# Score products of an attention kernel in four 64x64 array tiles instead of two 64x128 tiles

## The chip, the cores and the metric

The kernel runs on one core of one Trainium2 chip. The metric is the device time of one execution in microseconds (us), lower is better. The core has a matrix engine (TensorE, PE in the profile, with its weight loads listed apart as PEld), three engines for elementwise work (VectorE or DVE, ScalarE or ACT, GpSimd or POOL) and SyncE (SP), which issues DMAs. A matmul on TensorE uses two instructions: a weight load, which puts the stationary operand into the array, and the matmul itself, which streams the moving operand past it. Results go to PSUM.

## The reference

Attention with a sliding window of 128 positions and a linear distance bias, for 8 batches, 8 heads, 576 positions and head size 64; then layer norm, a two-layer MLP and a residual sum:

```python
scores = (1 / sqrt(64)) * q @ k.T                 # per batch and head, 576 x 576
scores = where(0 <= rel < 128, scores - slope[h] * abs(rel), -1e9)
attn = softmax(scores)
x = (attn @ v) with heads joined                  # 8 x 576 x 512
xn = (x - mean) / sqrt(var + 1e-6) * g_ln
out = x + maximum(xn @ w_ch1, 0) @ w_ch2          # 512 -> 2048 -> 512
```

All inputs and the output are fp32; the kernel computes in fp16 with fp32 sums.

## The kernel before

The 8 x 576 positions are cut into 36 blocks of 128 rows. `attention(i)` does one block: it loads q, k and v as fp16 (casting DMAs from the GpSimd queue), turns q and k so that the head's 64 elements lie on partitions (`qkt`, tiles of 128 partitions x 2 x 4 x 128: two heads lie above one another, one on partitions 0 to 63, the other on 64 to 127, and four such pairs side by side), makes the scores (`e_s`, L732), takes their exponent on ScalarE out of PSUM (`e_x`, L780), masks them on VectorE (`e_m`, L787), multiplies with v (`e_pv`, L808, 65 columns: 64 of v and one of ones for the sum) and normalises on VectorE (L825, L829). Because of the window, a block's queries see only the keys of their own block and of the one before, so the scores of a block are 8 heads x 2 key blocks = 16 products of 128 keys x 128 queries with a contraction of 64. Blocks that start a batch have no block before and make 8.

The scores are written turned, keys on the partitions: the weights are 128 keys of one head (64 rows x 128 columns), the moving operand is the 128 queries of that head, and the result fills 128 partitions of the score tile. The two score tiles (`sc0`, `sc1`, two PSUM banks each) take four heads each. The innermost loop goes over the two heads `g` of a pair: their operands lie on different halves of the partitions, and their results in different PSUM banks. For the first five blocks the distance bias is laid into PSUM by a matmul first (`e_z`, L748) and the score product adds to it (`start=not bias`); later blocks multiply with a mask table instead.

`mlp(c)` does the MLP for chunks of two or four blocks: the first layer at L1210 (at L1121 for the last two chunks), the second at L1247 for the first four chunks and at L992 for the others; L1121 and L992 follow a scheme with fewer products and more sums. Both use the four general PSUM tiles `fb`.

The order of all work is written out by hand: `ORDER` (L119 to L210) is a list of task names with the engine and the PSUM tile of each, `plan.run()` turns it into a list of closures, and each engine executes its share in that order. `S7:T0` in it is the score task of block 7 on TensorE. A score task holds all 16 products of a block (`Sa` and `Sb` hold half each for the first two blocks); score tasks stand between MLP tasks and value tasks (`pva`, `pvb`), so that the score matmuls come in short blocks among others. Waits are placed by the framework: a score task waits for the turned q and k (for most blocks a transposing DMA on SyncE's queue, L710) and for ScalarE to have read the score tile of the block before. `keep_warm` (L1287) puts in idle matmuls at the start.

Of the kernel before, what the change touches and what calls it, by code (L numbers as in the profile page):

```python
# [213 lines left out]
def kernel(  # L214
# [10 lines left out]
    nc = tc.nc  # L225
    B, H, S, D = q.shape
# [3 lines left out]
    P = 128  # L230
# [57 lines left out]
    def ring(name, n, shape, dt, pinned=()):  # L288
        return plan.ring([sb(f"{name}{i}", shape, dt) for i in range(n)], {k: sb(f"{name}p{k}", shape, dt) for k in pinned})
# [20 lines left out]
    qkt = ring("qkt", 6, [P, 2, HP, P], FP16, FAR)  # L310
# [33 lines left out]
    scs = [spsum.tile([P, 2, 512], FP32, tag=f"sc{n}", name=f"sc{n}") for n in range(2)]  # L344
# [216 lines left out]
    def attention(i):  # L561
# [4 lines left out]
        bias = i < BY_BIAS  # L566
# [155 lines left out]
        def e_s(halves):  # L722
            def emit(e, b):
                for half in halves:
                    for slot in range(2):
                        hp = 2 * half + slot
                        for side in (() if r == 0 else (0,)) + (1,):
                            for g in range(2):
                                rows = slice(D * g, D * g + D)
                                kt = qkt[i if side else before]  # L730
                                c0 = slot * 2 * P + side * P
                                nc.tensor.matmul(  # L732
                                    scs[half][:, g, c0 : c0 + P],
                                    kt[rows, 1, hp, :],
                                    qkt[i][rows, 0, hp, :],
                                    start=not bias,
                                    stop=True,
                                    skip_group_check=True,
                                )
            return emit  # L740

        def e_z(halves):
# [587 lines left out]
```

## Time and profile before

| What | us |
|---|---|
| Median of 3 runs (lowest, highest) | 300.7 (299.6, 300.96) |
| The profiled execution, whole | 300.98 |
| Its span from first to last instruction | 299.1 |
| VectorE busy | 242.8 |
| ScalarE busy | 165.3 |
| GpSimd busy | 105.4 |
| L732 weight loads, busy | 14.9 + 2.3 |

The page of a profile gives the busy time of each engine, the chain of work that ended last (followed back from the last instruction to what released each step), and groups of instructions by source line: how many, how long they kept the engine busy together, and the mean duration of one. Matmuls are pipelined: one of 128 columns is listed with 216 ns, but the next can start 56 ns behind it. So durations of single matmuls do not add up, and the steps between their starts are what tells the cost. A timeline row gives the start, the length and the number of instructions that were merged into it. The granted TensorE clock is full from 14.5 us of the span on; between 11.1 and 14.5 us it is half.

The 16 DMA engines are busy for nine tenths of the time or more in nearly every slice until about 190 us of the span, for the most part with the casting loads.

### The profile page before, as it was taken

The numbers are of one execution on the slowest core, as the hardware profiler recorded it, in microseconds if no ns is written. First come the engines' busy times: TensorE is split into PE (matmuls) and PEld (weight loads), VectorE is DVE, ScalarE is ACT, GpSimd is POOL, SyncE is SP. The second block draws the span as 40 slices with busy tenths as digits, with TensorE's granted clock in tenths as the row PEclk, the third lists the DMA queues.
The fourth block names the chain that finished last, engine by engine and source line by source line (L and its number), as shares of the span: only waits on it lengthen the run. The fifth ranks groups of instructions, "written<-read, shape, count | busy, mean of one in ns | idle before, by whom it ended". The sixth has DMA issues, their size and how long they took to land.

```text
span 299.1 us, 7458 instructions
## 1 busy us (share of the span) xinstructions
PE 293.3 (98%) x3014; PEld 225.1 (75%) x3014; DVE 242.8 (81%) x583; ACT 165.3 (55%) x273; POOL 105.4 (35%) x138
## 2 busy tenths in 40 slices
PE   8999999999999999899999999999999999999995
PEld 8789756875955578566886588657787799999984
DVE  3397289998879879849978888788899988988983
ACT  3664536794798573368528444676544655245500
POOL 5965369738137428433633567300000000000000
PEclk9799999999999999999999999999999999999999
DMA  6999999999999999999999999968101033012015
GB/s 179 159 196 194 206 144 141 146 138 133 122 219 145 151 224 133 145 140 167 179 166 197 182 159 143 158 171 150 36 19 55 0 125 89 2 37 106 35 55 193
DMA packets 163779, 39.93 MB, mean 133 GB/s; under 512 B 154017, under 2 KB 159137, under 8 KB 163746
## 3 DMA queue, kind: packets, MB, share of 16 engines
q0 software_dynamic: 110000, 17.70, 95.6%
q1 hardware_dynamic: 53744, 21.77, 40.5%
q8 instruction: 23, 0.38, 0.6%
q14 instruction: 10, 0.08, 0.1%
q10 hardware_dynamic: 2, 0.00, 0.0%
HBM read 36.70 MB, written 9.44 MB: 154 GB/s over the span
## 4 chain that ended last, share of the span: by engine, by line
PE 94%; DMA 4%; DVE 1%; ACT 0%; issue 0%
PE fb L1210 32%; PE fb L992 27%; PE fb L1247 9%; PE u L1121 8%; PE sc L732 6%; PE fb L808 6%; DMA qkt<-qk 4%; PE fb L1287 2%; PE sc L748 1%; PE fb L695 1%; PE fb L440 0%; PE fb L906 0%; PE fb L426 0%; DVE ot L1004 0%; DVE xb L829 0%; ACT probs L780 0%
## 5 line engine op out<-in xcount | busy, mean ns | idle before, releaser
L1210 PE MATMUL fb<-xt,w1sb 128*128 128x512 f16 (+1 forms) x576 | 106.4, 332 | 0.6 <-DMA xt<-xs 0.6
L780 ACT ACTIVATE probs<-sc 128x1024 f16<-128x1024 f32 (+1 forms) x72 | 67.4, 975 | 36.0 <-PE sc L732 27.3
L1210 PEld LDWEIGHTS <-w1sb 128*128 128x128 f16 x576 | 61.5, 114 | 27.8 <-DMA xt<-xs 0.9
L1227 ACT ACTIVATE ht<-fb 128x512 f16<-128x512 f32 x88 | 51.1, 598 | 44.4 <-PE fb L1210 44.2
L992 PEld LDWEIGHTS <-ht 128*128 128x128 f16 x560 | 53.2, 98 | 9.2
L496 POOL DMA_DIRECT2D qk<-in_k_dram x38 | 32.8, 866 | 44.3 <-DMA qkt<-qk 36.8
L992 PE MATMUL fb<-w2sb,ht 128*128 128x256 f16 x336 | 44.7, 273 | 0.0
L496 POOL DMA_DIRECT2D qk<-in_q_dram x38 | 32.5, 861 | 16.6 <-DMA qkt<-qk 9.6
L496 POOL DMA_DIRECT2D vx<-in_v_dram x36 | 31.0, 868 | 15.6 <-PE fb L808 12.4
L787 DVE TENSOR_TENSOR probs<-probs,mreg 128x1024 f16<-128x1024 f16 (+1 forms) x46 | 30.4, 667 | 1.1 <-ACT probs L780 1.0
L992 PE MATMUL fb<-ks,ht 128*128 128x256 f16 x224 | 30.8, 273 | 0.0
L1247 PE MATMUL fb<-w2sb,ht 128*128 128x512 f16 x128 | 30.7, 379 | 0.0
L829 DVE SCALAR_TENSOR_TENSOR xb<-fb,rec 128x256 f16<-128x256 f32 x72 | 29.5, 416 | 0.9
L808 PEld LDWEIGHTS <-probs 128*128 128x128 f16 x544 | 23.9, 98 | 6.8
L808 PE MATMUL fb<-vx,probs 128*128 128x65 f16 x496 | 26.1, 194 | 0.0
L1004 DVE TENSOR_TENSOR ot<-fb,xb 128x512 f32<-128x512 f32 (+1 forms) x31 | 19.6, 634 | 6.0 <-PE fb L992 5.6
L848 DVE BATCH_NORM_STATS2 st<-xb 128x6 f32<-128x512 f16 x36 | 24.2, 682 | 0.2
L825 DVE RECIPROCAL rec<-fb 128x4 f32<-128x4 f32 x72 | 12.2, 174 | 14.7 <-PE fb L808 12.4
L1225 DVE TENSOR_SCALAR ht<-fb 128x512 f16<-128x512 f32 x24 | 16.0, 681 | 8.4 <-PE fb L1210 8.3
L1247 PEld LDWEIGHTS <-ht 128*128 128x128 f16 x128 | 11.6, 98 | 11.1
L732 PEld LDWEIGHTS <-qkt 64*128 64x128 f16 x496 | 14.9, 94 | 6.4 <-issue 5.3
L1144 DVE TENSOR_TENSOR ht<-u,probs 128x512 f16<-128x512 f32 x24 | 16.2, 685 | 2.7 <-PE u L1121 1.8
(113 smaller groups left out, 387.7 us busy)
## 6 DMA issues: line engine op xcount, KB each, us to landing
out_dram<-ot SPq DMA_DIRECT2D x32, 256.0 KB, 2.9
qk<-in_q_dram POOLq DMA_DIRECT2D x30, 128.0 KB, 7.6
qk<-in_k_dram POOLq DMA_DIRECT2D x30, 128.0 KB, 7.2
vx<-in_v_dram POOLq DMA_DIRECT2D x28, 128.0 KB, 7.7
w1sb<-in_moe_w_ch_dram POOLq DMA_DIRECT2D x4, 512.0 KB, 9.1
w2sb<-in_moe_w_ch_dram POOLq DMA_DIRECT2D x4, 512.0 KB, 14.1
out_dram<-ot SPq DMA_DIRECT2D x8, 128.0 KB, 1.8
qs<-in_q_dram SPq DMA_DIRECT2D x2, 256.0 KB, 3.6
```

What stands on the lines that cost most here:

```text
L496: nc.gpsimd.dma_start(out=dst(p0, n), in_=src[b, :, s0 : s0 + n, :].rearrange("h p d -> p h d"))
L732: nc.tensor.matmul(scs[half][:, g, c0 : c0 + P], kt[rows, 1, hp, :], qkt[i][rows, 0, hp, :], start=not bias, stop=True, skip_group_check=True,
L780: nc.scalar.activation(out=o, in_=n_, func=AF.Exp, scale=inv_sqrt_d)
L787: en.tensor_tensor(out=pv, in0=pv, in1=mask[:, 2 * half : 2 * half + 2, :, lo:], op=ALU.mult)
L808: nc.tensor.matmul(pp[:, hh * (D + 1) : hh * (D + 1) + D + 1], probs[i][:, bank, slot, side * P : side * P + P], vx[i if side else before] ...
L829: nc.vector.scalar_tensor_tensor(out=xb[c][:, j, 256 * half : 256 * half + 256].rearrange("p (h d) -> p h d", d=D), in0=pp[:, :, 0:D], sca ...
L848: nc.vector.bn_stats(out=st[i][:, :], in_=xb[c][:, j, :])
L992: nc.tensor.matmul(o, lhs(f, p), rhs(f), start=first and f == 0 and (p == 0 or key[0] != key[1]), stop=f == F2 - 1, skip_group_check=True)
L1121: nc.tensor.matmul(late[bank][:, FOURTH * f : FOURTH * f + FOURTH], w, rhs[kb], start=first and f == kb == 0, stop=kb == 1, skip_group_che ...
L1210: nc.tensor.matmul(fb[b][:, n_ * x : n_ * x + n_], w1f[f // CB][:, kb, (f + x) % CB, :], xt[c][:, kb, 0:n_], start=(kb == x == 0), stop=(k ...
L1227: nc.scalar.activation(out=o, in_=src, func=AF.Relu)
L1247: nc.tensor.matmul(pm[:, 0 : c1 - c0], ht[c][:, f, j * P : j * P + P], w2sb[f // CB][:, f % CB, c0:c1], start=(f == 0), stop=(f == NFB - 1),)
```

## The change

The weights of one score product, 64 rows x 128 key columns, are loaded and used in two halves of 64 key columns. Each half is a matmul of its own with the same moving operand (the head's 128 queries), and writes 64 of the 128 result partitions. With the two heads of a pair that makes four products on four 64x64 quarters of the array: rows 0 to 63 or 64 to 127 by the head, columns 0 to 63 or 64 to 127 by the half of the keys. Their order is head 0 low keys, head 0 high keys, head 1 low keys, head 1 high keys. 544 score matmuls and as many weight loads become 1088 of each; results, tiles, waits and the order of the tasks stay.

```diff
                                 c0 = slot * 2 * P + side * P
-                                nc.tensor.matmul(
-                                    scs[half][:, g, c0 : c0 + P],
-                                    kt[rows, 1, hp, :],
-                                    qkt[i][rows, 0, hp, :],
-                                    start=not bias,
-                                    stop=True,
-                                    skip_group_check=True,
-                                )
+                                for z in range(2):
+                                    nc.tensor.matmul(
+                                        scs[half][D * z : D * z + D, g, c0 : c0 + P],
+                                        kt[rows, 1, hp, D * z : D * z + D],
+                                        qkt[i][rows, 0, hp, :],
+                                        start=not bias,
+                                        stop=True,
+                                        skip_group_check=True,
+                                    )
```

`D` is 64 and `P` is 128.

## Prediction

> **What bounds the kernel now.** I read the busy shares first, then the chain that ended last, then TensorE's own waits, then the score products' line.
>
> ```profile
> PE 293.3 (98%) x3014; PEld 225.1 (75%) x3014; DVE 242.8 (81%) x583; ACT 165.3 (55%) x273; POOL 105.4 (35%) x138
> ...
> PE 94%; DMA 4%; DVE 1%; ACT 0%; issue 0%
> PE fb L1210 32%; PE fb L992 27%; PE fb L1247 9%; PE u L1121 8%; PE sc L732 6%; PE fb L808 6%; DMA qkt<-qk 4%; PE fb L1287 2%; PE sc L748 1%; PE fb L695 1%; PE fb L440 0%; PE fb L906 0%; PE fb L426 0%; DVE ot L1004 0%; DVE xb L829 0%; ACT probs L780 0%
> ```
>
> The page says that TensorE sets the end: 94% of the chain is matmuls, and L732, the score products, is 6% of it. TensorE executes in order, so what is added to one matmul group moves everything behind it, unless a wait swallows it. There is little to swallow it:
>
> ```profile
> PE fb L1287 <- DVE warm_t L387: 1.1, 1, 1.1
> PE fb L1210 <- DMA xt<-xs: 0.6, 1, 0.6
> PE sc L732 <- DMA qkt<-qk: 0.5, 1, 0.5
> PE fb L1287 <- DVE xb L829: 0.3, 1, 0.3
> ```
>
> These are TensorE's waits (total us, times, longest). The first lies ahead of any score product. Only the 0.5 us, at 125.1 us of the span, and the 0.6 us could absorb something. So a longer score block costs nearly its full length.
>
> One score block in the timeline (start us, us, what):
>
> ```profile
> 131.53 0.65 PE L808 MATMUL fb<-vx,probs 128*128 128x65 f16 x16
> 132.11 0.23 PE L732 MATMUL sc<-qkt,qkt 64*128 64x128 f16 x2
> 132.17 0.22 PE L732 MATMUL sc<-qkt 64*128 64x128 f16 x2
> 132.23 0.22 PE L732 MATMUL sc<-qkt,qkt 64*128 64x128 f16 x2
> ...
> 132.51 0.22 PE L732 MATMUL sc<-qkt 64*128 64x128 f16 x2
> 132.66 0.62 PE L1210 MATMUL fb<-xt,w1sb 128*128 128x512 f16 x2
> ```
>
> The two matmuls of a row (the two heads, rows 0-63 and 64-127) start together, 3 to 4 ns apart by the trace's start times, and the rows are 56 ns apart. So two 64x128 tiles already run side by side, and a pair costs one stream of 128 columns: 56 ns, which is 2.4 columns per ns plus a little over 2 ns. There are 544 such matmuls, that is 272 pairs, 15.2 us, in 37 blocks (31 of 16 matmuls, the rest of 4, 8 or 12). Around each block the trace has two gaps: 123 ns from the last L808 matmul to the first L732 one, where the L808 matmuls are 29 ns apart, so 94 ns extra; and 148 ns from the last L732 matmul to the next line's, where pairs are 56 apart, so 92 ns extra. 37 x 186 ns = 6.9 us go to these changes of array shape.
>
> **The change, part by part.**
>
> *What moves.* Only TensorE's stream differs: 544 matmuls and 544 weight loads become 1088 of each. The tasks' order and all other engines' work stay. No DMA, no wait and no buffer is added.
>
> *Streaming.* Each new matmul still streams 128 columns of queries. Four 64x64 tiles fill the array just as two 64x128 tiles did, so four matmuls that run side by side still need 56 ns: 272 x 56 ns, change 0. Less than 56 is excluded: the next four use the same tiles, and 128 columns at the 2.4 per ns seen here take 53. If the two key halves of one head took turns instead, it would be 2 x 56 = 112 per four.
>
> *Weight loads.* Each fp16 load of the trace has its 128 columns read as four strips of 32; the fp32 loads are one strip of 128. A 64-column load is none of the trace's shapes, so I bound it. From above, the fp32 loads of L440, whose matmuls have one column and cannot hide them:
>
> ```profile
> 8.68 1.12 PE L426 MATMUL fb<-ot 1*128 1x512 f32 x2
> ...
> 10.41 1.25 PE L440 MATMUL fb<-ot 1*128 1x1 f32 x8
> ```
>
> The L440 loads start about 110 ns apart, the two of L426 107 apart, and a stream of 512 fp32 columns in L426 took 427 ns. So one fp32 strip goes in at 1.2 columns per ns, and so does an fp32 stream; 64 columns at that rate are 53 ns. An fp16 stream here runs at twice the fp32 rate (2.4); if loads scale alike, 64 fp16 columns are 27 ns. From below: the first pair of a block takes 227 ns instead of 216 and the second starts 66 ns behind it instead of 56, so 10 to 11 ns of a four-strip load are bare. I take 27 (half-width elements, and load and stream had one rate in fp32).
>
> What of it lies beside the stream? Now, the next pair's loads are issued 2 ns after a pair starts and hide under its 56 ns. At a block's start both heads' loads begin 3 ns apart and the second head's second matmul is still only 4 ns behind the first's, so loads to different rows do not queue. For two column halves of the same rows there is no row. If they go in together, 27 ns hide under 56; if one after the other, 2 x 27 = 54 still just hide, perhaps with a few ns over (58 to 60 per four). I take 57: 272 x 1 ns = +0.3 us. Bounds: 0 to +1.1 us.
>
> *Edges.* At each block's start the bare load grows from 11 to 27 ns: 37 x 16 = +0.6 us. The fourth tile's last matmul starts 7 ns later than the second did: 37 x 7 = +0.3 us. The 92 and 94 ns of emptying I leave: they are alike after 64-row and 128-row matmuls, so they do not follow the rows used; whether they follow the columns no row shows. If half the columns saved 64 / 2.4 = 27 ns at the exit, it is -1.0 us, if at the entry too, -2.0.
>
> *Issue.* 64 instead of 32 instructions per block. At the wait of 125.1 us, four loads and two matmuls were issued within 18 ns of the release, 3 ns each; the new block needs 7 ns each. Cost 0, because the 56 ns of stream cover eight issues; without that cover (the 14 ns per instruction of today's block as the fastest rate) a four would be 112.
>
> *Given back.* 21 of the 37 blocks lie ahead of the 0.5 us wait. Their share of the extra, 0.7 us, could vanish in it, but the transfer waited for itself follows buffers that score products free. I count -0.2 us, at most -0.5.
>
> *Sum:* 0.3 + 0.6 + 0.3 - 0.2 = **+1.0 us**. The profiled execution took 300.98 us (span 299.1 and 1.9 around it), which gives 302.0. It was 0.3 us above the median of the runs (300.7), so I forecast **301.7 us**: no change that counts. About 0.5% (1.5 us, 299.2 to 302.2) is what a measurement of this kernel can tell from none. With its bounds the case reaches from 300.1 (loads +0, exits -1.0, 0.5 given back: -0.6 in all) to 303.7 (loads +1.1, a bare 53 ns load at each block's start, 37 x 42 ns = +1.6, the later last start +0.3, nothing given back: +3.0).
>
> **A rule against the change.** The Trainium skill, "TensorEngine Tiling (Array Packing)", section "Restrictions and Gotchas", says that column tiling cannot be combined with the fast weight load; "TensorE: Matmul & The Clock Gate", section "LDWEIGHTS (loading the stationary operand)", prices a plain load at columns / 1.2, that is 53 ns for 64. The four strips of 32 in the trace fit the first. By the second, two loads per row half are 107 ns, and the sum would be rival 2's; the fp32 rows agree with 1.2, but no fp16 row does, and I stay with 27.
>
> **Rivals.**
>
> 1. *The load no longer hides under the same tile's stream.* Then a tile alternates, 56 + 27 = 83 per four: 272 x 27 = 7.3, plus the edges' 0.7 net: +8.0, **308.7 us**. It decides as soon as the first matmuls of consecutive fours are 80 ns apart. For it: two more tiles share the rows' supply of weights and operands. Against it: today a load is issued 2 ns after a matmul on the same rows, and pairs stay 56 apart. (The skill's TensorE page, Part 3, "The mechanism", says that a load overlaps a running matmul of other row groups only, or goes to a background buffer; the present pairs show the latter for full width.)
>
> 2. *Tiles take turns.* Either the two column halves stream one after the other (112 per four), or their loads queue at the fp32 rate (2 x 53 = 107), or all four load-and-matmul steps go singly as the 65-column L808 ones do, 29 ns each (117). 272 x (51 to 61) = +13.9 to +16.6, plus 0.7: **315.3 to 318.0 us**; 317 as its value. This is also the case in which the change does not do what it says: four tiles on paper, two at work. For it: no row of this trace has a tile narrower than 128 columns. Against it: the two row tiles do run together.
>
> 3. *All four loads queue at 53 ns:* 213 per four, 272 x 157 = +42.7, **344 us**. Against it: loads to different rows do not queue today.
>
> 4. *Faster.* The array empties sooner with half the columns, 27 ns at both edges of each block, and loads stay covered at the entry too: 37 x 54 = -2.0, plus 0.3 for the later last start: -1.7, **299.0 us**. It needs both edges; one alone stays inside the 0.5%. For it: 6.9 us lie at these edges, the only time that four narrower tiles could shorten. Against it: the emptying did not change with half the rows.
>
> **How the numbers follow.** The forecast has 0.50, rival 1 0.17, rival 2 0.21, rival 3 0.06, rival 4 0.06. Of the forecast's 0.50, 0.08 lies above 302.2 (fours at 59 or 60, uncovered entries). Faster 0.06, same 0.42, slower 0.08 + 0.17 + 0.21 + 0.06 = 0.52. So slower as a whole is likelier than no change, but it is spread over three mechanisms, and none of them is as likely as the hidden load. The range leaves out rivals 3 and 4, 0.12 together: 300.0 to 318.0. The forecast's own range is 300.1 to 303.7.
>
> **What would show it.** In the timeline of the new kernel, the step between fours: 56 to 60 is the forecast, about 83 rival 1, 107 to 117 rival 2, over 200 rival 3. Within a four, starts 3 to 4 ns apart show four tiles side by side; two pairs some 27 or 56 ns apart show queued loads or streams. The gap in front of a block after L808 should be 123 to 140 ns, and the gap behind it near 148; 120 would be rival 4. The number of L732's records doubles to 1088, the 0.5 us wait for the transposed load shrinks, and VectorE and ScalarE keep their busy times. The forecast is wrong if the 64-column load costs more than half the stream: then every ns over 56 per four is 0.27 us.

## The result and the profile after

| | Before | After |
|---|---|---|
| Median of 7 runs (lowest, highest), us | 300.96 (299.6, 301.13) | 301.9 (301.17, 302.29) |
| Profiled execution, us | 300.98 | 302.0 |
| Its span, us | 299.1 | 300.2 |
| Last matmul's start to the end of the span, us | 3.51 | 3.98 |

The ratio is 1.0044, with a 95% interval from 1.003 to 1.0059: slower by 0.9 to 1.8 us, clear of zero, with its middle inside the 0.5% that the prediction had set as "no change that counts" and its upper end just above it. The forecast was 301.7.

The page of the changed kernel, with the lines that answer to those shown of before:

```profile
PE 294.5 (98%) x3558; PEld 227.0 (76%) x3558; DVE 242.8 (81%) x583; ACT 165.3 (55%) x273; POOL 104.8 (35%) x138
...
PE 98%; DVE 1%; issue 0%
PE fb L1211 33%; PE fb L993 29%; PE fb L1248 9%; PE u L1122 8%; PE sc L733 7%; PE fb L809 6%; PE fb L1288 2%; PE sc L749 1%; PE fb L695 1%; PE fb L647 0%; PE fb L907 0%; PE fb L426 0%; PE fb L440 0%; DVE ot L1005 0%; DVE xb L830 0%
```

544 matmuls and 544 weight loads more, VectorE and ScalarE as before, and TensorE still sets the end (code behind the edit has its line numbers moved by one). One score block:

```profile
131.83 0.65 PE L809 MATMUL fb<-vx,probs 128*128 128x65 f16 x16
132.41 0.25 PE L733 MATMUL sc<-qkt,qkt 64*64 64x128 f16 x4
132.49 0.23 PE L733 MATMUL sc<-qkt 64*64 64x128 f16 x4
132.54 0.23 PE L733 MATMUL sc<-qkt,qkt 64*64 64x128 f16 x4
...
132.82 0.23 PE L733 MATMUL sc<-qkt 64*64 64x128 f16 x4
132.98 1.92 PE L1211 MATMUL fb<-xt,w1sb 128*128 128x512 f16 x8
```

Each row now holds four matmuls, one on each of the four tiles ("a four" from here on), where it held a pair, and the rows are as far apart as before, but for the first step: 132.41 to 132.49 instead of 132.11 to 132.17. The starts of this block in both traces, in ns from the last value matmul (L808, L809):

```
            first   step to 2nd   later steps   within a row   last start to next line   whole block
before      124     66            56            0, 3..4        148                       677
after       121     80            56            0, 4, 7, 10    149                       695
```

TensorE's waits changed their place:

```profile
PE fb L1288 <- DVE warm_t L387: 1.1, 1, 1.1
PE fb L1211 <- issue: 0.6, 1, 0.6
PE fb L1288 <- DVE xb L830: 0.3, 1, 0.3
```

The two waits for transposing DMAs are gone. A wait that the page calls "issue", for nothing that it can name, is new (0.6 us of idle time; 0.73 by the starts of the matmuls on either side). Compared matmul by matmul, the changed kernel's last matmul starts 0.57 us later than that of before. The parts: 36 score blocks together 0.65 us longer (16 to 27 ns each, 18 in the middle; the 37th is the one behind the wait at 125.1 us); the new wait 0.73; the two gaps that ended on DMAs -0.80 and -0.51; the rest, 0.5, is the slow start: up to 5.38 us of the span instead of 4.29, the idle matmuls of `keep_warm` come 107 ns apart and not 56, and at half speed half of the 1.09 us more is lost. From there to the end of the span it is another 0.47 us, after the last score product is long done. The block is what the prediction was about. The wait and the end were not in it.

### The profile page after: what moved, and what is told of

Same layout as the page of the kernel before. It is cut to its first block, busy times and chain, and to the rows that moved or that the text cites. A ratio compares the mean times of both kernels' runs of the same rounds, so it can differ in the third digit from the quotient of the medians.

```text
span 300.2 us, 8546 instructions
## 1 busy us (share of the span) xinstructions
PE 294.5 (98%) x3558; PEld 227.0 (76%) x3558; DVE 242.8 (81%) x583; ACT 165.3 (55%) x273; POOL 104.8 (35%) x138
## 4 chain that ended last, share of the span: by engine, by line
PE 98%; DVE 1%; issue 0%
PE fb L1211 33%; PE fb L993 29%; PE fb L1248 9%; PE u L1122 8%; PE sc L733 7%; PE fb L809 6%; PE fb L1288 2%; PE sc L749 1%; PE fb L695 1%; PE fb L647 0%; PE fb L907 0%; PE fb L426 0%; PE fb L440 0%; DVE ot L1005 0%; DVE xb L830 0%
## 5 line engine op out<-in xcount | busy, mean ns | idle before, releaser
L809 PEld LDWEIGHTS <-probs 128*128 128x128 f16 x544 | 23.9, 98 | 6.7
L809 PE MATMUL fb<-vx,probs 128*128 128x65 f16 x496 | 26.1, 194 | 0.0
L733 PEld LDWEIGHTS <-qkt 64*64 64x64 f16 x992 | 16.2, 107 | 6.4 <-issue 5.3
```

The costliest lines, as they stand in the source:

```text
L733: nc.tensor.matmul(scs[half][D * z : D * z + D, g, c0 : c0 + P], kt[rows, 1, hp, D * z : D * z + D], qkt[i][rows, 0, hp, :], start=not bia ...
L809: nc.tensor.matmul(pp[:, hh * (D + 1) : hh * (D + 1) + D + 1], probs[i][:, bank, slot, side * P : side * P + P], vx[i if side else before] ...
```

## The experiments

Theory A/H: four tiles load and stream side by side; the cost is a longer first load of each block and the later start of the fourth tile. Rival Q: the loads of the two halves of one head go one after the other and only just hide. Rival B, later S: the longer instruction stream itself costs time outside the blocks. Ratios are to the kernel before, run on the same chip beside each.

### The kernel before, again

No edit.

> The kernel before, unchanged, against itself. It measures how far two equal kernels differ here, and gives a second profile. Theory A (the cost lies in the score blocks alone): the waits outside the score blocks move between two profiles of one kernel by some tenths of a us, ratio 1.000 within 0.0015. Theory B (the longer instruction stream delays the start or the stretch between blocks in every execution): the stretch from the first instruction to the first score block is the same in both profiles of this kernel, within 0.1 us.

300.46 us, ratio 0.9994 (0.9979 to 1.0009). The blocks repeat within 3 ns, but for the one behind the wait at 125.1 us and one near 13 us, at half clock. The stretch ahead of the first score block does not: it was 0.78 us longer than in the first profile. The full speed came at 5.92 us instead of 4.29, and half of that difference is 0.8. So a later start in one profile is no finding, and Theory B's first half falls. Both waits for transposes are absent here (-0.80 and -0.53). TensorE came 0.85 us later to that place, but that is not what ended them: the transfers landed at 119.14 and 121.66 us of the span instead of 121.37 and 125.04. In the two profiles of the changed kernel it was 119.56 and 121.17, 119.35 and 121.72. A TensorE as early as in the first profile, at the first place at 120.6 and at the second at 123.8 us, would have found them done too. So the two waits belong to that one execution's transfers.

### The changed kernel, again

No edit.

> The changed kernel, unchanged, a second time. Theory A: each of the 37 score blocks is again 17 to 19 ns longer than before, +0.67 us in all, and nothing else is common to both profiles of the changed kernel; ratio 1.001 to 1.004. Theory B: the first score block starts 0.5 us later again and the wait of about 0.7 us between 80 and 88 us is there again; ratio 1.004 to 1.006.

302.65 us, ratio 1.0059 (1.0036 to 1.0082). The blocks again: +16 to +19 ns, 18 in the middle, but for the same two. The "issue" wait near 80 us is absent. The first score block starts 1.23 us later, with full speed from 6.88 us. The end is there: 3.89 us from the last matmul to the end of the span, against 3.51 and 3.49 in the two profiles of before. So the ratio fits Theory B and B's wait is not there, while A's "nothing else is common" falls with the longer end. The middle of this interval lies above 0.5%, that of the first comparison below it.

### Another order of the four tiles

```diff
-                            for g in range(2):
+                            for z, g in ((0, 0), (0, 1), (1, 0), (1, 1)):
...
-                                for z in range(2):
```

> The four tiles in another order: low keys of both heads, then high keys of both heads, so that neighbours in the stream lie on different rows. Theory H (loads of all four tiles go in side by side): nothing changes, 56 ns from four to four, first step 80 ns, time as the changed kernel's, 302. Theory Q (two column halves of the same rows load one after the other): the first step falls towards 66 to 70 ns or the steps within a four move apart differently, up to 37 x 14 ns = 0.5 us faster than the changed kernel, 301.4.

302.29 us, ratio 1.0044 (1.0024 to 1.0064). The same steps to the ns: 80, then 56, starts 3 to 4 ns apart within a four. The order in which rows and columns alternate is of no account, as H has it.

### Half of the tiles at a time

```diff
-                for half in halves:
+                for z, half in ((z, half) for z in range(2) for half in halves):
...
-                                for z in range(2):
```

> All products of the low key halves of a block first, then all of the high halves, so that only two of the four tiles have work at a time. Theory H (four tiles are free only because all four stream side by side): 56 ns per pair of narrow tiles, 272 more pairs, +15.2 us, time 316. Rival (a narrow matmul is cheaper than a wide one, its step falls to 28 to 40 ns): 301 to 307.

309.2 us, ratio 1.0281 (1.025 to 1.0313): +8.5 us, between the two. The block in the timeline:

```profile
136.87 0.24 PE L732 MATMUL sc<-qkt,qkt 64*64 64x128 f16 x2
136.95 0.22 PE L732 MATMUL sc<-qkt 64*64 64x128 f16 x2
137.01 0.22 PE L732 MATMUL sc<-qkt,qkt 64*64 64x128 f16 x2
137.06 0.22 PE L732 MATMUL sc<-qkt 64*64 64x128 f16 x2
137.12 0.25 PE L732 MATMUL sc<-qkt,qkt 64*64 64x128 f16 x4
...
137.28 0.25 PE L732 MATMUL sc<-qkt 64*64 64x128 f16 x4
137.37 0.22 PE L732 MATMUL sc<-qkt,qkt 64*64 64x128 f16 x2
```

Four rows of two, four rows of four, four rows of two, all 56 ns apart but for the first step: a narrow pair is as dear as a wide one, so the rival falls, and without four at work the price of a row is paid for half the products. But in the middle the high halves run while the low ones are still under way. In ns, the ninth pair of the program starts 9 ns behind the fifth (137.127 against 137.118), then takes a first step of 80 of its own and steps of 56, interleaved with pairs five to eight. So a block has 12 steps instead of 16 and is 268 ns longer than before, where 16 steps would be some 450. So a matmul need not wait for those that stand ahead of it in the program and are queued on another tile: the ninth pair passed pairs six to eight. It passed no more than these three: its two tiles stood idle for the first four rows. No run shows why; pairs one to four write to the same PSUM tile as pairs nine to twelve, and it may also be the number of instructions that TensorE looks ahead. The Trainium skill, "TensorEngine Tiling (Array Packing)", section "Tiling Modes", says that different tiles can do their loads and matmuls in parallel; this trace agrees, in the four rows of four.

### 64 queries per matmul, two wide tiles

```diff
-                            for g in range(2):
+                            for y, g in ((y, g) for y in range(2) for g in range(2)):
...
-                                c0 = slot * 2 * P + side * P
+                                c0 = slot * 2 * P + side * P + 64 * y
...
-                                    scs[half][:, g, c0 : c0 + P],
+                                    scs[half][:, g, c0 : c0 + 64],
...
-                                    qkt[i][rows, 0, hp, :],
+                                    qkt[i][rows, 0, hp, 64 * y : 64 * y + 64],
```

> The two wide tiles of before, but the 128 queries streamed in two matmuls of 64, with the weights loaded for each. It halves the cover that a load has. Stream 64 / 2.4 + 2.3 = 29 ns per pair; a four-strip load of 10 to 13 ns stays hidden: 58 instead of 56 ns per old pair, +0.7 us, time 301.6. If loads and not streams set the step: more than 32 ns per pair, over 303.

301.92 us, ratio 1.0035 (1.001 to 1.0061). 29 ns per pair, 20 ns more per block, as expected. This kernel has as many TensorE instructions as the changed one and wide tiles; it has an "issue" wait of 0.3 us at 81.4 us too, and 4.11 us at the end. So those two do not come from the narrow tiles. (A wait of 0.5 us at 168.2 us, by the page for a load of v, is in this profile too.)

### 64 queries per matmul, four narrow tiles

```diff
-                            for y, g in ((y, g) for y in range(2) for g in range(2)):
+                            for y, g, z in ((y, g, z) for y in range(2) for g in range(2) for z in range(2)):
...
-                                    scs[half][:, g, c0 : c0 + 64],
-                                    kt[rows, 1, hp, :],
+                                    scs[half][D * z : D * z + D, g, c0 : c0 + 64],
+                                    kt[rows, 1, hp, D * z : D * z + D],
```

> The four narrow tiles, queries streamed in two matmuls of 64 (29 ns of cover). Theory H (the four loads go in side by side, 27 ns): still hidden, 29 to 31 ns from four to four, at most 62 per old four, +0.7 to +2.3 us, time 302 to 303. Theory Q (loads of the two column halves of the same rows go one after the other, 2 x 27): 54 ns from four to four, 108 per old four, +14 us, time 315. If the supply of instructions limits (16 per old pair's 56 ns, 128 per block): first fours at 29, later ones slower.

314.97 us, ratio 1.048 (1.0438 to 1.0523). Rival Q's number came out, but not its mechanism: the rows are not 54 but 32 ns apart.

```profile
142.43 0.26 PE L732 MATMUL sc<-qkt,qkt 64*64 64x64 f16 x8
142.52 0.23 PE L732 MATMUL sc<-qkt 64*64 64x64 f16 x8
142.58 0.23 PE L732 MATMUL sc<-qkt,qkt 64*64 64x64 f16 x8
142.65 0.23 PE L732 MATMUL sc<-qkt 64*64 64x64 f16 x8
```

A row merges two fours, and 65 ns from row to row are 32 per four (the wide pairs had 29). So the four loads do go in side by side, and they set the step now. The supply of instructions does not set it here: the four matmuls of a step and the loads behind them all start within 12 ns, and then nothing starts for 19. The block is 87 ns longer than before, some 3 us in all. Of the other 11 us, 7.0 are in two rows of TensorE's waits:

```profile
PE fb L1210 <- issue: 4.6, 2, 2.6
PE sc L732 <- issue: 2.4, 3, 1.1
```

and the largest of them:

```profile
57.91 1.80 PE L1210 MATMUL fb<-xt,w1sb 128*128 128x256 f16 x15
62.28 0.49 PE L1210 MATMUL fb<-xt,w1sb 128*128 128x256 f16 x3 [2.56 <-issue]
```

Matmuls of the MLP whose operands were long there stand still for 2.6 us. What arrives at that time is an instruction packet. The page's row of that queue, of the kernel before, of the changed one and of this one:

```profile
q8 instruction: 23, 0.38, 0.6%
```

```profile
q8 instruction: 28, 0.46, 0.7%
```

```profile
q8 instruction: 36, 0.59, 0.9%
```

13 packets of 16 KB more than before for 3264 more TensorE instructions, some 65 bytes each: these packets are TensorE's program, 256 instructions at a time. In this kernel the five steps of over 0.45 us between matmul starts behind 20 us of the span end 1.61, 1.64, 1.58, 1.68 and 1.44 us after a packet has landed. The issue wait of the changed kernel ended 1.51 us after one:

```profile
80.64 0.85 PE L1211 MATMUL fb<-xt,w1sb 128*128 128x256 f16 x6
82.05 0.38 PE L1211 MATMUL fb<-xt,w1sb 128*128 128x256 f16 x2 [0.56 <-issue]
```

with the packet taken at 79.02 us and landed at 80.54. Those of the other kernels near 80 us ended 1.42 (the other order), 1.35 (64 queries, wide) and 1.52 us (narrow tiles early, below) after theirs. The reading is that TensorE ran out of program. It rests on these times and on the count of packets; no run moved a packet alone.

### 32 queries per matmul, four narrow tiles

```diff
-                            for y, g in ((y, g) for y in range(2) for g in range(2)):
+                            for y, g, z in ((y, g, z) for y in range(4) for g in range(2) for z in range(2)):
...
-                                    qkt[i][rows, 0, hp, 64 * y : 64 * y + 64],
+                                    qkt[i][rows, 0, hp, 32 * y : 32 * y + 32],
```

> The four narrow tiles, queries streamed in four matmuls of 32 (16 ns of cover), so that the load must come out. Theory H: the step is the bare load, 24 to 29 ns from four to four, 96 to 116 per old four, +11 to +16 us, time 312 to 317. Theory Q: 54 per four, 216 per old four, +43 us, time 344. If a 64-column load costs no more than a four-strip one (10 to 13 ns): 16 ns per four, +2 us, 303.

375.98 us, ratio 1.2487 (1.2425 to 1.2548). Two rows of a block, of four fours each, lie 130 ns apart:

```profile
181.19 0.28 PE L732 MATMUL sc<-qkt 64*64 64x32 f16 x16
181.32 0.28 PE L732 MATMUL sc<-qkt,qkt 64*64 64x32 f16 x16
```

So while instructions last it is 32 ns from four to four, as with 64 queries: half the stream changes nothing, so this step is the load's. It is above the 24 to 29 that H gave and far from Q's 54. H's time of 312 to 317 is missed by 59 us, because H did not count the program: there are 20 waits for instructions, up to 5.3 us, ending 1.2 to 1.8 us behind a packet, and the granted clock was 0.95 over the span against 0.99 before. In the blocks, once the instructions held ready are used up, matmuls start 8 to 9 ns apart, each with its load: some 4.2 ns per instruction.

### One array shape throughout

```diff
-                                    kt[rows, 1, hp, :],
-                                    qkt[i][rows, 0, hp, :],
+                                    kt[:, 1, hp, :],
+                                    qkt[i][:, 0, hp, :],
```

> Score products over all 128 rows, one matmul of 128 rows x 128 columns where one of 64 rows stood, so that the array keeps one shape throughout. Each result is then the sum of two heads' products instead of one head's. No two matmuls run side by side any more: 56 ns each, 272 more steps, +15.2 us. If the 94 and 92 ns around a block are the change of shape, they vanish: 37 x 186 ns = -6.9 us, sum +8.3, time 309. If they are there for another reason (the wait on the semaphore, the switch between PSUM tiles): 316.

307.52 us, ratio 1.0226 (1.0199 to 1.0254): +6.8 us.

```profile
135.28 0.27 PE L732 MATMUL sc<-qkt,qkt 128*128 128x128 f16 x2
135.39 0.28 PE L732 MATMUL sc<-qkt 128*128 128x128 f16 x2
...
136.06 0.28 PE L732 MATMUL sc<-qkt 128*128 128x128 f16 x2
136.17 0.38 PE L1210 MATMUL fb<-xt,w1sb 128*128 128x512 f16 x1
```

The gaps at both ends are gone: 29 ns from the last value matmul to the first score product (123 before), 56 from the last score product to the next line (148). So the 94 and 92 ns were the change of shape, as the prediction read them. Blocks are 244 ns longer, 7.9 us in all without the one behind the DMA wait, and the two DMA waits are gone again.

### Narrow tiles early or late only

```diff
+                                w = D if i < 22 else P
+                                for z in range(P // w):
+                                    nc.tensor.matmul(
+                                        scs[half][w * z : w * z + w, g, c0 : c0 + P],
+                                        kt[rows, 1, hp, w * z : w * z + w],
```

and with `i >= 22`.

> Four narrow tiles only in the score blocks 0 to 21 (up to about 155 us of the span), two wide ones after. Theory S (besides 18 ns per block, the change costs a wait for TensorE's own instructions, whose transfers of 16 KB fall behind near 80 us of the span): 23 blocks x 18 = +0.4 us, and in the profile a gap of 0.3 to 0.8 us between 73 and 83 us that ends 1.3 to 1.7 us after an instruction packet has landed; ratio 1.002 to 1.005. Rival R (the rest lies nowhere in particular): no such gap, ratio about 1.0027 (three fifths of 1.0044).

301.54 us, ratio 1.0036 (1.0012 to 1.006). There is a gap of 0.23 us more at 81.2 us, smaller than expected, which ends 1.52 us behind a packet.

> Four narrow tiles only in the score blocks 22 to 35. Theory S: 14 blocks x 18 = +0.25 us and no gap near 80 us, since the instructions up to there are those of the kernel before; ratio 1.000 to 1.002. Rival R: ratio about 1.0017 and no gap either, so that this run tells by its sum with the other one.

301.05 us, ratio 1.0011 (0.9987 to 1.0036), and no gap. The places fit Theory S, but the two intervals overlap, so the totals alone do not decide between S and R. Neither kernel has the longer end (3.49 and 3.51 us).

### The bare loads

Two wide tiles with 32 queries:

```diff
-                            for y, g in ((y, g) for y in range(2) for g in range(2)):
+                            for y, g in ((y, g) for y in range(4) for g in range(2)):
...
-                                    qkt[i][rows, 0, hp, 64 * y : 64 * y + 64],
+                                    qkt[i][rows, 0, hp, 32 * y : 32 * y + 32],
```

> The two wide tiles, the queries in four matmuls of 32 (16 ns of cover), to lay bare the four-strip load of 128 columns. The run with narrow tiles and 32 queries had 32 ns from four to four, and 32 with 64 queries too, so that 32 ns is what the 64-column loads take. If a four-strip load is as much shorter as its strips (32 against 64 columns): 16 to 19 ns per pair. If a wide load takes as long as a narrow one: 32 ns per pair, and the narrow loads have no price of their own. With 64 matmuls and 64 loads per block waits for instructions come on top as they did with 64 queries in narrow tiles, 303 to 315.

One execution, without an interval: 319.14 us, some 12 us of it from blocks that are 344 ns longer, and 4.1 us from waits for instructions. 25 ns per pair, between the two expectations. So a pair with four-strip loads of 128 columns can follow after 25 ns, a four with one-strip loads of 64 columns only after 32. Whether the 25 is the load or the least step of a matmul as short as this, no run tells: none streams 32 columns without such a load.

Eight tiles with 32 key columns each:

```diff
-                                for z in range(2):
+                                for z in range(4):
...
-                                        kt[rows, 1, hp, D * z : D * z + D],
+                                        kt[rows, 1, hp, 32 * z : 32 * z + 32],
```

> Eight tiles of 64x32: loads of 32 columns, one strip. Theory H (tiles stream and load side by side, the load is one strip at its own length): first step of a block 66 to 70 ns instead of 80, since the strip is as long as one of a four-strip load; then 56 ns per eight while instructions last. 128 matmuls and 128 loads per block are more than are held ready: from about a third of the block on 8 to 9 ns per matmul and load, 67 to 70 ns per eight, and waits for instructions as in the run with 32 queries in narrow tiles; 330 to 380. If the first step stays 80, the extra length is not the load's.

One execution: 315.96 us. A block has 64 matmuls and 64 loads, not the 128 that the expectation says, so its 330 to 380 was too high.

```profile
143.11 0.25 PE L733 MATMUL sc<-qkt,qkt 64*32 64x128 f16 x8
143.18 0.24 PE L733 MATMUL sc<-qkt 64*32 64x128 f16 x8
143.23 0.24 PE L733 MATMUL sc<-qkt,qkt 64*32 64x128 f16 x8
```

The first step is 66 to 67 ns, as before and not 80: a strip of 32 columns is bare for as long as four strips of 32 side by side. Then there are two steps of 56 ns per eight and one of 75; with the 33rd matmul of a block the starts go over to 8 to 9 ns per matmul with its load, 67 per eight. So the first step follows the length of the strip.

### The end

From the start of the last matmul to the end of the span, and when the last instruction packet was taken:

```
kernel                        span end   last packet before the last matmul
before, twice                 3.51 3.49  more than 8 us
one shape                     3.51       more than 8 us
64 queries, four tiles        3.50       more than 8 us
narrow early / late           3.49 3.51  6.87 / 8.00 us
eight tiles, 32 queries (2)   3.50 3.51 3.49  more than 8 us
changed, twice                3.98 3.89  2.78 / 3.18 us
other order                   4.25       3.12 us
64 queries, two tiles         4.11       3.14 us
half of the tiles at a time   3.78       2.82 us
```

The five profiles of kernels whose program ends with a 28th packet have it 2.8 to 3.2 us ahead of the last matmul, among the last output transfers, and end 0.3 to 0.75 us later; the nine others lie between 3.48 and 3.52. That the packet delays the output transfers is argued from the times; no run moved the packet alone.

## Why the prediction was right

*Streaming* (change 0): right. 56 ns from four to four, in every block at full clock of both profiles.

*Weight loads* (+0.3 us, 0 to +1.1): 0. Four loads go in side by side and hide. The 27 ns were about right: the bare first load is 24 (a step of 80 against 56), and with the cover taken away the step is 32 ns. The two halves one after the other, 54, is refuted by the 32. Of the rule against the change that the prediction quotes from the Trainium skill, the trace agrees with the first part: it has the 64 columns as one strip. The price of 53 ns is not met; by it the fours with 32 queries would be 53 ns or more apart, and they are 32 apart.

*Edges* (+0.6 and +0.3): right in kind. The first load costs +14 ns per block instead of +16, the fourth tile +7 as forecast, and the first score product comes 2 to 3 ns earlier. That is 18 ns per block, 0.65 us together against 0.9. The emptying stayed at 148 ns with half the columns used, so rival 4 had no ground.

*Issue* (0): this is the step that failed. The argument was the rate at which instructions leave the queue, and within a block that held: 64 instructions at 7 ns each. It left out that the program itself has to be brought in. 1088 more instructions are five more packets of 16 KB, and TensorE waited 0.73 us for one in one profile of the changed kernel and not at all in the other. By the starts of its matmuls it waited 0.2 and 0.4 us in two other kernels with narrow tiles up to there, and not at all in the one with half of the tiles at a time. A further 0.4 to 0.5 us are the longer end. The sum counted neither.

*Given back* (-0.2): the two waits did vanish, but not because longer blocks filled them: their transfers landed earlier. They are absent from a second profile of the kernel before as well, so no saving is shown.

The sum of the measured terms, 0.65 for the blocks, 0.4 to 0.5 for the end and 0 to 0.7 for the wait, is 1.05 to 1.85 us; the interval is 0.9 to 1.8. The stream, the hidden loads and the edges are the mechanism that was forecast, and it held. That the sum of +1.0 came so close to the measured +0.9 is partly luck: loads and edges were put some 0.55 us too high and 0.2 us was given back, while the instruction stream, at 0, was 0.4 to 1.2 us too low. *Rivals 1 to 3* fall with the step of 56; rival 2's turns appear only where the program leaves two tiles without work. No experiment with an edit was faster than the kernel before.

## What to carry to other kernels

Splitting tiles that already fill the array bought nothing here: the stream sets the step, and narrower tiles only add instructions. Read the step between starts, not the duration of one matmul, and ask in a dense block whether the load still hides under the shortest stream. Count instructions of the whole program as well as of the block: a gap that the page calls "issue" and that ends some 1.5 us behind a packet of the instruction queue is most likely TensorE out of program, and with 3264 more instructions such gaps cost more than the longer blocks (7.0 us against 3). A wait seen in one profile alone is looked for in a second one of the same kernel before anything is built on it.

## What the runs showed that was not expected

- A tile's matmuls start ahead of earlier ones of the program that queue on another tile: the ninth pair 9 ns behind the fifth, with three pairs of the two other tiles between them in the program.
- The change of array shape costs 94 ns going in and 92 coming out, the same with 64 or 128 columns per tile, and nothing else in the block explains them: without it the steps are 29 and 56 ns.
- In the kernel with 64 queries and four tiles, behind a wait for instructions of 2.0 us that ended at 70.95 us, matmuls of 512 columns came 426 ns apart instead of 216 for some 3 us: the granted clock was half from 71.9 to 75.3 us. A long wait can so be paid twice. But no half clock followed the wait of 2.56 us that ended at 62.28 us, so the length of the wait alone does not decide it.
- The same kernel's time before the first score block differed by 0.78 us between two profiles, with full speed from 4.29 or from 5.92 us of the span. Below 0.3% one profile says little on a total, while the blocks at full clock repeat within 3 ns.
